# A spectral mixer gated by a token MLP: a buffer for PSUM copies, the order of ScalarE and VectorE before the last stage, and the place of one transform

## The chip, the cores and the metric

The kernel runs on one core of a Trainium2 chip. A core has a matrix engine (TensorE, "PE" in the profile), whose weight loads run beside its matmuls ("PEld"), a vector engine (VectorE, "DVE"), a scalar engine (ScalarE, "ACT"), a general engine (GpSimd, "POOL") and a queue engine (SyncE, "SP"). Each engine works through its own instructions in order; between engines there are only semaphores. SP and POOL also issue the DMA transfers. The metric is the device time of one execution in microseconds; the median over runs is compared.

## The reference

The input is x, 2048 tokens by 512 channels, fp32. It is normalized over the channels once. Two branches start from there: a filter in the Fourier domain over tokens and channels, and an MLP over the tokens (with a second normalization ahead of it). The second branch gates the first.

```python
xn = _layernorm(x, axis=-1)
# filter
X = jnp.fft.rfft2(xn, axes=(-2, -1)) * (w_r + 1j * w_i)
s = jnp.fft.irfft2(X, s=(S, D), axes=(-2, -1))
# token MLP: S = 2048 -> F = 1792 -> S
h = _layernorm(xn, axis=-1)
u = _gelu(jnp.einsum("bsd,sf->bdf", h, w1) + b1)
g = _silu((jnp.einsum("bdf,fs->bds", u, w2) + b2).transpose(0, 2, 1))
return x + s * g
```

## The kernel before

**Tiling.** Token s sits in partition s // 16 and in row j = s % 16, so x is 16 rows of 128 x 512. The Fourier transform over tokens is split into one of length 128 (matmuls against a table) and one of length 16 over the rows. Products of the MLP are made in two parts, high and low, of fp32 values: three matmuls stand for one product (high by high, high by low, low by high). The high part is a rounding copy on ScalarE, the low part a subtraction on VectorE.

**First stage (lines 456 to 520).** The loop over 16 rows makes, in row j, the products of seven of the fourteen 128-wide groups of hidden features with the row's h (line 395; `hidden_early`, lines 392 to 400, four groups to PSUM banks 0 to 3, then three to banks 4 to 6). Between the second and third pass of the first four groups stands `between()`: the row's transform of length 128, four matmuls into bank 7 (`first_transform`, lines 223 to 227). ScalarE copies bank 7 out (`first_copy`, line 231), and `fold` (lines 234 to 250) adds and subtracts pieces of the copy zt into the columns of ey: o, e and two halves of t on VectorE, two groups of ey on GpSimd, one copy of o to the other half of the partitions on ScalarE (line 244), the other two groups of ey on VectorE (line 247). `fold` is a generator: `first_copy` of row j is issued at the end of row j, its folds a row later. For the last row they are issued behind the loop, at line 520, behind the gelus of groups 2 and 1 and behind the first high and low parts of the next weights.

**Middle stage (lines 525 to 751).** The other seven groups and the filter are interleaved by a string of steps, `STEPS`; each letter advances one stream. The first step of the filter is `along_channels`, four matmuls per unit (line 586) that read ey and write bank 4 + q; the units run in the order q = 3, 2, 1, 0. Banks 4, 5 and 6 hold products of the first stage until their gelus have read them.

**Take-over to the last stage (lines 754 to 849).** The last four groups' products still run on TensorE, four parts at a time: `rest(units, gelu)` issues units of products and then the gelu of the group that they complete. Meanwhile the weights w2 of the last stage are loaded and split into high and low parts. The last product is a Strassen-like scheme of seven products for each of eight pairs of output rows (j, j + 8), in the order 1, 2, 5, 6, 3, 7, 4. For each product there is a weight form (`w2_forms`, lines 783 to 812; `w2_form` is one ScalarE copy and one VectorE subtraction, 128 x 896 each): form 1 from the tile a12, 2 from a11, 5 from s1, 6 from s1 + a12, 3 from that + a11, 7 from s4, 4 from a21. On the other side the hidden values u of group pair i, four quarters, are split and summed by `forms(i)` (lines 302 to 327) in five steps: fd (form 1), fa (forms 2 and 3), four sums on VectorE, fc (forms 6 and 5), fb (forms 4 and 7). The last two pairs, 5 and 6 (`last` and `last6`), are made at the take-over. There `strict` is set, and `ordered` keeps an instruction behind the one that was written before it for the same engine. An instruction that is not kept can be put by the scheduler wherever its engine would otherwise stand idle.

**Last stage (lines 854 to 978).** Product n of pair p adds up 21 matmuls (line 941) in one of the banks `bx`, `by`, `bz`. `copied` (line 894) copies a bank's partial sum out on ScalarE, because the next product goes on adding into the same bank: products 1, 6, 7 and 4 share `bx`, and p1 is what stood there after product 1. `sequence` (line 866) and `channels` (line 875) are the last transforms of the filter, `gate` the silu, `finish` the last multiplication and the write.

**Buffers.** Tiles come from pools, which lie on a left and a right side of the memory; a pool that is opened where another was closed lies over its tiles, and each tile then waits for the last readers of the tiles that it overlaps. The pool "us" holds the three tiles u of the hidden values, "w1" the weights of the first two stages; "fin", of the last stage, lies over both. Its first tile is p1. The pool "w2" lies over the middle stage's "mid".

**Loads.** `s1`, `a12`, `a11`, `s4`, `a21` are 448 KB pieces of w2 (line 764); s1 and s4 are sums of two pieces, the second added by a DMA that accumulates (line 766, issued by POOL). The pieces of the next pair are loaded into the same tiles as soon as those are read.

Of the kernel before, what the change touches and what calls it, by code (L numbers as in the profile page):

```python
# [8 lines left out]
F32 = mybir.dt.float32  # L9
# [109 lines left out]
def spectral_mixer_kernel(tc, x, w1, b1, w2, b2, wk, we, wx, c_f, c_ft, c_d, c_i, c_g, c_h, c_s, out):  # L119
# [22 lines left out]
    with tc.tile_pool(name="ps", bufs=1, space=PSUM) as psp, ExitStack() as left, ExitStack() as right:  # L142
# [80 lines left out]
        def first_transform(h, c):  # L223
            z = ps[:, 7].rearrange("p (b c) -> p b c", c=P)
            for b in range(4):
                T.matmul(z[:, b], h[:, b * P:(b + 1) * P], c, start=True, stop=True)  # L226
            return z
# [58 lines left out]
        def gelu(ft, bank):  # L286
            i, half = ft % NH, ft // NH
            if i not in raw:
                raw[i] = usp.tile([P, 2, D], F32, name=f"u{i}", tag="u")
            ordered(A.activation(raw[i][:, half], ps[:, bank], AF.Gelu_apprx_tanh, bias=b1t[:, ft:ft + 1]))  # L290
# [101 lines left out]
        def hidden_early(j, nf, bank, w, between):  # L392
            def products(wi, hj, first, last):
                for i in range(nf):
                    T.matmul(ps[:, bank + i], w[wi][:, i * P:(i + 1) * P], hj, start=first and j == 0, stop=last and j == NJ - 1)  # L395
            products(0, hh[j], True, False)
            products(1, hh[j], False, False)
            r = between()
            products(0, hl[j], False, True)
            return r  # L400
# [56 lines left out]
        for j in range(NJ):  # L457
            more = j + 1 < NJ
            if more:
                raws[j + 1, 0], raws[j + 1, 1] = w1_load(j + 1, *WA), w1_load(j + 1, *WB)  # L460
            if j == 0:
                load_x(3)
                load_x(4)
                SY.dma_start(b1t, b1)
                SY.dma_start(b2t, b2)
            if j == 4:
                SY.dma_start(cd, c_d)
                G.dma_start(cft, c_ft)
            if j in (6, 8, 10, 12):
                q = slice(16 * (j - 6), 16 * (j - 4))  # L470
                SY.dma_start(out[q, :NJ - 1], x[q, :NJ - 1])
            z = hidden_early(j, 4, 0, w[0], lambda: first_transform(h, c))
            hidden_early(j, 3, 4, w[1], lambda: None)

            early = j > 0
            if more:
                w = w1_tiles(j + 1, *WA), w1_tiles(j + 1, *WB)
                h = new_h(j + 1)
                normed(h, xs[j + 1], *of[j + 1])
                high(hh[j + 1], h)  # L480
                if early and j + 3 < NJ:
                    stats(of[j + 3][0], of[j + 3][1], xs[j + 3])
                    if j % 2 == 0:
                        spreads(of[j + 2][0], 2)
            for _ in range(3):
                next(folds, None)
            if more:
                high(w[0][0], raws[j + 1, 0])
            next(folds, None)
            if more:  # L490
                if early and j % 2 == 0 and j + 2 < NJ:
                    scales(of[j + 2][0])
                low(w[0][1], raws[j + 1, 0], w[0][0])
                if not early:
                    stats(m, 0, xs[2])
                high(w[1][0], raws[j + 1, 1])
                low(hl[j + 1], h, hh[j + 1])
                c = turned(j + 1, *of[j + 1])
                if not early:
                    stats(m, 1, xs[3])  # L500
                    spreads(m, 2)
            run(folds)
            if more:
                low(w[1][1], raws[j + 1, 1], w[1][0])
                if not early:
                    scales(m)
                if j % 2 == 0 and j + 4 < NJ:
                    m = moments(f"m{j + 4}", 2)
                    of.update({j + 4: (m, 0), j + 5: (m, 1)})
            if j + 5 < NJ:  # L510
                load_x(j + 5)
            folds = fold(j, first_copy(j, z))
            if j == NJ - 2:
                for i in range(3):
                    w1_raw(i)
        gelu(2, 2)
        w1_high(0)
        w1_low(0)
        gelu(1, 1)
        run(folds)  # L520
        w1_high(1)
        rstage.close()

# [229 lines left out]

        V, A, G, SY = free
        w2p = pool(right, "right", "w2", 3)
        NP, HD = NJ // 2, D // 2
        ORDER = (1, 2, 5, 6, 3, 7, 4)

# [24 lines left out]
        def w2_forms():  # L783

            for p in range(NP):
                yield w2_form(f"1_{p}", cur["a12"])
                yield w2_form(f"2_{p}", cur["a11"])
                w = w2_form(f"5_{p}", cur["s1"])
                ordered(V.tensor_add(cur["s1"], cur["s1"], cur["a12"]))
                yield w  # L790
                w = w2_form(f"6_{p}", cur["s1"])
                if p == 0:
                    yield w
                if p + 1 < NP:
                    nxt["s1"] = s1_load(p + 1, (w2p, fp)[(p + 1) % 2])
                    nxt["a12"] = w2_load("a12", w2p, p + 1, 1)
                if p:
                    yield w
                V.tensor_add(cur["s1"], cur["s1"], cur["a11"])  # L799
                w = w2_form(f"3_{p}", cur["s1"])  # L800
                if p + 1 < NP:
                    nxt["a11"] = w2_load("a11", w2p, p + 1, 0)
                yield w
                w = w2_form(f"7_{p}", cur["s4"])
                if p + 1 < NP:
                    nxt["s4"] = w2_load("s4", w2p, p + 1, 1, (p + 1 + NP, 1))
                yield w
                w = w2_form(f"4_{p}", cur["a21"])
                if p + 1 < NP:
                    nxt["a21"] = w2_load("a21", fp, p + 1 + NP, 0)  # L810
                    cur.update(nxt)
                yield w
# [2 lines left out]

        wforms = w2_forms()
        strict.append(True)
        ready = [next(wforms) for _ in range(3)]

        def rest(units, *gelus):  # L820
            for _ in range(units):
                next(streams["h"])
            for _ in gelus:
                next(streams["g"])
        rest(SPLIT, 5)
        rest(4, 12)
        last, last6 = forms(5), forms(6)
        next(last)
        next(last)
        rest(4, 13)  # L830
        rest(4, 6)
        next(last6)
        next(last)
        next(last6)
        next(last6)
        next(last)
        next(last6)
        ready.append(next(wforms))
        run(last)
        run(last6)  # L840
        strict.clear()
        lstage.close()
        fp = pool(left, "left", "fin", 1)
        HW = [P, HD]
        made = {"p1_0": fp.tile(HW, F32, name="p1_0", tag="p1")}
        gs = [fp.tile([P, D], F32, name=f"g{j}", tag="g", bufs=3) for j in (0, NP)]
        made["c11_0"] = fp.tile(HW, F32, name="c11_0", tag="c", bufs=2)
        made["od0"] = fp.tile([P, 2, P], F32, name="od0", tag="od")
# [43 lines left out]
            return y  # L892

        def copied(name, src):
            t = made.pop(name, None) or fp.tile([P, HD], F32, name=name, tag=name.split("_")[0])
            A.activation(t, src, AF.Copy)  # L896
            return t

# [117 lines left out]
```

## Time and profile before

| | us |
|---|---|
| median of 3 runs | 381.93 |
| lowest, highest | 381.85, 384.48 |
| the profiled execution | 382.29 |
| its span, from the first to the last instruction | 380.5 |
| TensorE busy in it | 369.8 |
| VectorE busy | 309.0 |
| ScalarE busy | 213.3 |
| GpSimd busy | 102.3 |

The profile is one execution, and all its times count from the start of its span. Several views of it are used below: the page with sums by engine; the waits, where a line names the waiting engine and line of code, the engine and line that released it, the total, the number of times and the longest; stretches of time with the busy time of each engine; and the timeline, one line for one or more like instructions in a row, with start, length, engine, line, operation, the tiles written and read, and in brackets the idle time before it and what ended it. "SPq" and "POOLq" are the queues of the two engines that issue DMAs. Lines in a helper that records every operation of an engine are shown as L128. The matmuls overlap, so the end of a row of them is modelled.

The three stages by these times: the first stage to about 98 us, the middle stage to 204.5, the last to the end.

### The profile page before, as it was taken

How to read it: one execution, taken by the hardware profiler on the slowest of the kernel's cores; microseconds unless marked ns; L12 is line 12 of the kernel's file. 1: busy time of each engine (PE TensorE's matmuls, PEld its weight loads, DVE VectorE, ACT ScalarE, POOL GpSimd, SP SyncE). 2: the span in 40 equal slices, each digit the busy share in tenths (PEclk: the TensorE clock that was granted, in tenths of full speed). 3: DMA queues.
4: the chain of work that ended last, by engine and by line, in shares of the span. 5: the costliest groups of instructions: out<-in, count | busy, mean ns of one | idle time of the engine just before them, and what ended most of it. 6: DMA issues, size and time to landing. Idle time of an engine off the chain costs nothing.

```text
span 380.5 us, 7482 instructions
## 1 busy us (share of the span) xinstructions
PE 369.8 (97%) x2760; PEld 327.8 (86%) x2760; DVE 309.0 (81%) x660; ACT 213.3 (56%) x384; POOL 102.3 (27%) x133
## 2 busy tenths in 40 slices
PE   8999999999999999999999799999999999999994
PEld 4888888888877676777779799999999999999994
DVE  5899999865799999999967798776767768777763
ACT  4677755754972365865456765545555555545541
POOL 2133233243511735765400011020303020200100
PEclk9999999999999999999999999999999999999999
DMA  7956467214455767999866599898888888895602
GB/s 249 323 190 231 133 222 239 91 42 128 120 196 179 253 213 258 283 280 307 194 181 155 149 267 188 265 164 263 168 246 184 223 204 193 194 217 158 100 0 56
DMA packets 41945, 73.32 MB, mean 193 GB/s; under 512 B 4180, under 2 KB 25172, under 8 KB 41780
## 3 DMA queue, kind: packets, MB, share of 16 engines
q1 hardware_dynamic: 35460, 58.88, 48.6%
q0 software_dynamic: 6448, 13.96, 21.4%
q8 instruction: 21, 0.34, 0.4%
q14 instruction: 16, 0.13, 0.1%
HBM read 60.24 MB, written 8.13 MB: 180 GB/s over the span
## 4 chain that ended last, share of the span: by engine, by line
PE 86%; DVE 8%; issue 2%; ACT 2%; DMA 1%; SPq 0%; DVEq 0%; ACTq 0%
PE ps L941 34%; PE ps L395 19%; PE ps L678 6%; PE ps L679 5%; PE ps L226 4%; PE ps L687 4%; PE ps L866 4%; PE ps L586 4%; PE ps L875 4%; DVE pq L128 2%; DVE e L128 2%; PE ps L665 1%; PE ps L681 1%; PE ps L600 1%; DMA x<-in_x_dram 1%
## 5 line engine op out<-in xcount | busy, mean ns | idle before, releaser
L395 PE MATMUL ps<-h,w1h 128*128 128x512 f32 x224 | 58.5, 398 | 0.0
L395 PEld LDWEIGHTS ps<-h,w1h 128*128 128x128 f32 x224 | 40.8, 188 | 8.1 <-ACT w1h L387 0.2
L776 DVE TENSOR_TENSOR w2f<-s,w2f 128x896 fp32r<-128x896 f32 x32 | 35.0, 1092 | 14.8 <-ACT w2f L775 13.7
L766 POOL DMA_DIRECT2D s<-in_w_dram x16 | 13.8, 865 | 122.7 <-DMA s<-in_w_dram 35.0
L678 PE MATMUL ps<-h,w1h 128*128 128x512 f32 x112 | 44.9, 401 | 0.0
L679 PE MATMUL ps<-h,w1h 128*128 128x512 f32 x112 | 43.7, 390 | 0.0
L941 PE MATMUL ps<-fb,w2f 128*128 128x256 f32 x336 | 42.9, 282 | 0.6 <-DVE c L904 0.6
L941 PE MATMUL ps<-fa,w2f 128*128 128x256 f32 x336 | 43.4, 283 | 0.0
L941 PE MATMUL ps<-fc,w2f 128*128 128x256 f32 x336 | 41.1, 279 | 2.1 <-ACT p L896 2.1
L941 PEld LDWEIGHTS ps<-fc,w2f 128*128 128x128 f32 x336 | 40.1, 188 | 2.3 <-ACT p L896 2.3
L941 PEld LDWEIGHTS ps<-fb,w2f 128*128 128x128 f32 x336 | 40.6, 188 | 1.4 <-issue 0.8
L941 PEld LDWEIGHTS ps<-fa,w2f 128*128 128x128 f32 x336 | 40.6, 188 | 0.0
L775 ACT ACTIVATE w2f<-s 128x896 fp32r<-128x896 f32 x32 | 30.3, 948 | 16.5 <-DVE s L799 13.5
L776 DVE TENSOR_TENSOR w2f<-a,w2f 128x896 fp32r<-128x896 f32 x24 | 26.1, 1089 | 15.8 <-ACT w2f L775 15.7
L128 POOL TENSOR_TENSOR s<-z,e 128x4 f32<-128x4 f32 x8 | 25.3, 3163 | 37.4 <-DMA z<-e 16.6
L775 ACT ACTIVATE w2f<-a 128x896 fp32r<-128x896 f32 x24 | 22.8, 950 | 21.7 <-PE ps L941 18.2
L395 PE MATMUL ps<-h,w1l 128*128 128x512 f32 x112 | 30.7, 390 | 0.1
L128 ACT ACTIVATE w1h<-w1s 128x512 fp32r<-128x512 f32 (+1 forms) x30 | 17.4, 581 | 22.2 <-PE ps L679 12.9
L678 PEld LDWEIGHTS ps<-h,w1h 128*128 128x128 f32 x112 | 21.0, 188 | 9.0 <-issue 5.0
L687 PE MATMUL ps<-h,w1l 128*128 128x512 f32 x93 | 25.6, 391 | 0.1
L395 PEld LDWEIGHTS ps<-h,w1l 128*128 128x128 f32 x112 | 20.9, 188 | 5.0 <-DVE w1l L390 0.5
L679 PEld LDWEIGHTS ps<-h,w1h 128*128 128x128 f32 x112 | 21.1, 188 | 4.0
(132 smaller groups left out, 730.8 us busy)
## 6 DMA issues: line engine op xcount, KB each, us to landing
a<-in_w_dram SPq DMA_DIRECT2D x24, 448.0 KB
s<-in_w_dram POOLq DMA_DIRECT2D x17, 448.0 KB, 7.0
s<-in_w_dram SPq DMA_DIRECT2D x15, 448.0 KB
w1r<-in_w_dram SPq DMA_DIRECT2D x16, 256.0 KB
z<-e SPq DMA_DIRECT2D x16, 256.0 KB
w1s<-in_w_dram SPq DMA_DIRECT2D x16, 256.0 KB
yj<-ey SPq DMA_DIRECT2D x16, 256.0 KB
x<-in_x_dram SPq DMA_DIRECT2D x15, 256.0 KB
```

Source lines behind the costliest of these rows:

```text
L128: return lambda *a, **k: keep(getattr(engine, name)(*a, **k))
L226: T.matmul(z[:, b], h[:, b * P:(b + 1) * P], c, start=True, stop=True)
L395: T.matmul(ps[:, bank + i], w[wi][:, i * P:(i + 1) * P], hj, start=first and j == 0, stop=last and j == NJ - 1)
L586: keep(T.matmul(pd[:, b * P:(b + 1) * P], ey[:, lo, b].rearrange("p h j -> p (h j)"), cd[:, b], start=True, stop=True))
L678: keep(T.matmul(o, wh[:, sl], hh[j], start=first, stop=False))
L679: keep(T.matmul(o, wh[:, sl], hl[j], start=False, stop=False))
L687: keep(T.matmul(ps[:, bank], wl[:, k * P:k * P + P], hh[j], start=False, stop=final))
L775: ordered(A.activation(wf[:, 0], v, AF.Copy))
L776: ordered(V.tensor_sub(wf[:, 1], v, wf[:, 0].bitcast(F32)))
L866: in_turn(j, T.matmul(pf[:, b], yj[:, b * P:(b + 1) * P], cft, start=True, stop=True))
L875: in_turn(j, T.matmul(pe[:, b % 2, b // 2], yt[:, b], ci[:, b], start=True, stop=True))
L941: in_turn(j0, T.matmul(o, wf[:, wi, i], ui, start=m + a == 0 and n in (1, 2, 5), stop=m == NH - 1 and a == 2, skip_group_check=n in (6, 3, ...
```

## The change

Three edits are in the diff.

1. In the last row of the first stage the transform is issued before the row's products instead of between them, and its folds are issued before the gelus of groups 2 and 1 instead of behind them.
2. p1, the copy of product 1's partial sum, gets a tile of its own in the pool "w2" (a 1 KB buffer per partition, the pool's first tile), for all eight pairs, and leaves "fin".
3. The order in which ScalarE's and VectorE's work is written at the take-over is another. Form 5 of w2 stands behind the gelu of group 5; the sums of u5 stand before the gelus of groups 13 and 6; the order behind the last gelu is fd6, fc5, fa6, then s1 + a12, the sums of u6, form 6 of w2, fc6, fb5, fb6. Before it was fd6, the sums of u5, fa6, the sums of u6, fc5, fc6, form 6, fb5, fb6, with s1 + a12 ahead of all of it. In `w2_forms` the sum s1 + a12 becomes part of the step of form 6, in every pair.

```diff
-            z = hidden_early(j, 4, 0, w[0], lambda: first_transform(h, c))
+            if more:
+                z = hidden_early(j, 4, 0, w[0], lambda: first_transform(h, c))
+            else:
+                z = first_transform(h, c)
+                hidden_early(j, 4, 0, w[0], lambda: None)
             hidden_early(j, 3, 4, w[1], lambda: None)
...
+        run(folds)
         gelu(2, 2)
         w1_high(0)
         w1_low(0)
         gelu(1, 1)
-        run(folds)
         w1_high(1)
...
         w2p = pool(right, "right", "w2", 3)
+        p1_0 = w2p.tile([P, D // 2], F32, name="p1_0", tag="p1", bufs=1)
...
-                w = w2_form(f"5_{p}", cur["s1"])
+                yield w2_form(f"5_{p}", cur["s1"])
                 ordered(V.tensor_add(cur["s1"], cur["s1"], cur["a12"]))
-                yield w
+                if p == 0:
+                    yield
                 w = w2_form(f"6_{p}", cur["s1"])
                 if p == 0:
                     yield w
...
-        ready = [next(wforms) for _ in range(3)]
+        ready = [next(wforms) for _ in range(2)]
...
         rest(SPLIT, 5)
+        ready.append(next(wforms))
         rest(4, 12)
         last, last6 = forms(5), forms(6)
-        next(last)
-        next(last)
+        for _ in range(3):
+            next(last)
         rest(4, 13)
         rest(4, 6)
         next(last6)
         next(last)
         next(last6)
-        next(last6)
-        next(last)
+        next(wforms)
         next(last6)
         ready.append(next(wforms))
+        next(last6)
         run(last)
         run(last6)
...
-        made = {"p1_0": fp.tile(HW, F32, name="p1_0", tag="p1")}
+        made = {"p1_0": p1_0}
...
-            t = made.pop(name, None) or fp.tile([P, HD], F32, name=name, tag=name.split("_")[0])
+            tag = name.split("_")[0]
+            t = made.pop(name, None) or (fp, w2p)[tag == "p1"].tile([P, HD], F32, name=name, tag=tag, bufs=1)
             A.activation(t, src, AF.Copy)
```

## The prediction

> **What bounds the kernel now.** The first view is the page: busy time of each engine in one profiled execution.
>
> ```profile
> span 380.5 us, 7482 instructions
> PE 369.8 (97%) x2760; PEld 327.8 (86%) x2760; DVE 309.0 (81%) x660; ACT 213.3 (56%) x384; POOL 102.3 (27%) x133
> ```
>
> TensorE is busy for 369.8 of 380.5 us, and the change removes no matmul. All that can be won is idle time of TensorE, 10.7 us in all, so the next view is its waits, and after it the busy time in stretches (columns: stretch, length, then PE, PEld, DVE, ACT and POOL busy, clock, DMA share, GB/s).
>
> ```profile
> PE ps L941 <- ACT p L896: 2.1, 1, 2.1
> PE ps L665 <- DVE pq L128: 1.2, 2, 0.7
> PE ps L586 <- DVE ey L247: 0.4, 1, 0.4
> ```
>
> ```profile
> 100.00:130.00 30.00, 29.87 (x227) 23.15 (x226) 29.36 (x52) 17.30 (x32) 8.92 (x11) 1.00 0.60 190
> 204.50:217.00 12.50, 10.39 (x88) 10.15 (x87) 10.15 (x18) 7.36 (x12) 0.86 (x1) 1.00 0.63 173
> 251.00:367.00 116.00, 116.00 (x989) 115.48 (x988) 86.40 (x166) 59.01 (x99) 17.43 (x20) 1.00 0.79 186
> ```
>
> Two of these waits lie where the diff works. The take-over to the last stage holds the largest, 2.1 us, for p1's copy; the start of the filter holds 0.4 us for the last columns of ey. Between the two VectorE is as full as TensorE (29.36 of 30), and behind 251 us TensorE never waits. A gain at either place can therefore be carried to the end by TensorE, if no new wait catches it.
>
> **The last row.** In time order, the end of the first stage (start, length, engine, line, tiles, count):
>
> ```profile
> 91.76 1.75 PE L395 MATMUL ps<-h,w1h 128*128 128x512 f32 x7
> 94.25 1.05 PE L226 MATMUL ps<-cf,h 128*128 128x128 f32 x8
> 95.34 0.60 ACT L231 ACTIVATE zt<-ps 128x512 f32<-128x512 f32 x1 [2.61 <-PE ps L226]
> 95.96 1.28 ACT L290 ACT_TABLE_LOAD   x1
> 97.07 0.46 DVE L240 TENSOR_TENSOR t<-o 64x128 f32<-64x128 f32 x1
> 97.25 1.27 ACT L290 ACTIVATE u<-ps,b1t 128x512 f32<-128x512 f32 x2
> 98.55 0.31 ACT L244 ACTIVATE o<-o 64x128 f32<-64x128 f32 x1
> 98.60 0.60 PE L586 MATMUL ps<-cd,ey 128*128 128x128 f32 x4
> 98.89 0.88 DVE L247 SCALAR_TENSOR_TENSOR ey<-t,o 128x128 f32<-128x128 f32 x2 [1.36 <-ACT o L244]
> 99.31 1.83 ACT L128 ACTIVATE u<-ps,b1t 128x512 f32<-128x512 f32 x3
> 99.57 1.63 PE L586 MATMUL ps<-cd,ey 128*128 128x128 f32 x12 [0.37 <-DVE ey L247]
> ```
>
> The seven matmuls at 91.76 are three of row 14 and the first four of row 15, at 0.227 each (1.59 to the next group, by 7), so row 15 begins at 92.44. Its transform now stands behind eight matmuls, at 94.25, and moves to 92.44: 1.81 earlier, its bank having been free since row 14's copy. The products keep their total. The copy zt goes from 95.34 to 93.53, and VectorE's last t ends at 97.53 − 1.81 = 95.72. The copy o, which now queues behind the table load and two gelus, follows at once (the folds stand ahead of the gelus in the new text) and ends near 96.05; L247 ends near 97.0 instead of 99.77. The wait at 99.57 goes. A 128-wide matmul takes 0.111 by this row of the chain that ended last:
>
> ```profile
> 217.04 0.89 PE ps L866 x8
> ```
>
> Four of L586 from 98.60 would reach 99.05, so the stall is worth 0.52.
>
> What is late next? ScalarE. The table load moves behind o, from 95.96 to 96.05; the two gelus end near 98.61 (98.52 before), the copy o (0.31, a step of 0.33 with its gap) no longer follows them, so the next gelus start at 99.07 instead of 99.31, 0.24 earlier. The second unit of L586 overwrites a bank that the first of those gelus reads; at 0.64 each (1.27 by 2) it ends at 99.71, while the matmuls would be ready at 99.49 (eight at 0.111). So 0.22 of the 0.52 turns into a new wait, and **0.3** is left. If the scheduler lets the first gelu pass o instead (its bank is ready near 95.9, o near 95.72), the load hides in the idle time behind zt and all 0.5 is won. I take 0.3, with ends 0 and 0.5, because the order of the text gives it. Nothing below zero: no work is added. Whether 0.3 lasts to 204 us depends on VectorE, which is full; its copies out of L586 and its forms move with TensorE and ScalarE by the same amount.
>
> [...]
>
> **The take-over.** The same view, some 100 us later:
>
> ```profile
> 203.45 0.33 SPq L764 DMA_DIRECT2D a<-in_w_dram  x1
> 203.83 1.38 SPq L853 DMA_DIRECT2D yj<-ey  x2
> 205.79 0.62 ACT L295 ACTIVATE fa<-u 128x512 fp32r<-128x512 f32 x1
> 205.93 0.42 DVE L296 TENSOR_TENSOR fd<-u,fd 128x256 fp32r<-128x256 f32 x1 [1.60 <-ACT fd L295]
> 208.70 0.42 DVE L315 TENSOR_TENSOR u<-u 128x256 f32<-128x256 f32 x1
> 209.65 2.63 PE L941 MATMUL ps<-fc,w2f 128*128 128x256 f32 x21
> 210.42 1.29 DVE L296 TENSOR_TENSOR fc<-u,fc 128x512 fp32r<-128x512 f32 x2
> 211.63 1.08 DVE L776 TENSOR_TENSOR w2f<-s,w2f 128x896 fp32r<-128x896 f32 x1
> 212.63 1.28 DVE L296 TENSOR_TENSOR fb<-u,fb 128x512 fp32r<-128x512 f32 x2
> 213.95 0.66 ACT L896 ACTIVATE p<-ps 128x256 f32<-128x256 f32 x2 [1.36 <-DVE fb L296]
> 214.39 2.65 PE L941 MATMUL ps<-fc,w2f 128*128 128x256 f32 x21 [2.11 <-ACT p L896]
> 214.43 0.86 POOL L766 DMA_DIRECT2D s<-in_w_dram  x1 [12.62 <-DVE fb L296]
> 215.94 1.09 DVE L776 TENSOR_TENSOR w2f<-s,w2f 128x896 fp32r<-128x896 f32 x1 [0.68 <-ACT w2f L775]
> 217.69 2.72 PE L941 MATMUL ps<-fa,w2f 128*128 128x256 f32 x21
> 218.74 0.58 ACT L868 ACTIVATE yt<-ps 128x512 f32<-128x512 f32 x1
> ```
>
> Product 6 of pair 0 (214.39) adds into the bank of product 1, so it waits for p1's copy. That copy waits for the last fb at 213.91: p1_0 lies where u of tile 6 lay. The other inputs of product 6 were there at 212.71 (its weights, L776). With p1_0 in w2's pool the copy needs only product 1, done long before, and its place: its tile comes first in its pool and lies over middle-stage tiles last used before 200 us, and the pool's other tiles keep theirs.
>
> *The buffer alone.* Product 6 starts at 212.75, 1.64 earlier. Product 3 (217.69, which is 3.30 after product 6, a transform between) would be ready at 216.05, but its weights are done at 217.03 and the third matmul needs them, 0.24 in: it starts near 216.8. Gain 0.9.
>
> *The new order.* From 205.93 VectorE's queue was fd6, four sums of u5, fa6, four sums of u6, fc5, fc6, w2f 6, fb5, fb6, L799. Now u5's sums stand before gelu 13 and run while VectorE waited (1.60 us idle before 205.93), and the sum s1 + a12, which ran ahead of this window, takes their room. With steps of 0.60 for a 512-wide form, 1.01 for an 896-wide one and 1.72 for four sums (208.70 to 210.42): fc5 follows ScalarE at 206.43, fa6 207.03, s1 + a12 207.63, u6's sums 208.64, w2f 6 210.36 (done 211.44), fc6 211.37 (done 212.06), fb5 and fb6 to 213.26, L799 213.17, then ScalarE's copy and w2f 3 at about 215.3, 0.65 before the 215.94 of now. Product 5 uses fc6's low part in its twentieth matmul, at 209.65 + 19/21 of 2.63 = 212.03: a new wait of under 0.1. Product 6 starts at 212.35, two us earlier. Product 3 is ready at 215.65 and waits for w2f 3, done 216.39, to near 216.15 in its first matmul: **1.5 gained**. Behind it the next in line is yt at 218.74, whose ScalarE queue moves by the same 0.65 and ends at 218.67; its reader comes behind product 3, some 2.5 on, at 218.65. That just fits. The upper end is the whole wait, 2.1; the lower end is 0.9, the buffer alone.
>
> *Other edits, at nothing.* w2f 5 behind one gelu is needed only at 209.65. In the other seven pairs the sum s1 + a12 is issued one product later, with no VectorE work between in the text; two products (2.63 each) cover it, and without that cover it would cost 1.08 a pair. fin is 1 KB shorter and its tiles slide; the u and w1 tiles below are dead by then in either place. The load of the next a12 must wait for the moved sum: 208.7 instead of 203.45, past yj and s on SP's queue. It is first read by pair 1's forms, behind the yt of 218.74 on ScalarE, some 10 us after.
>
> **The sum.** 0.3 + 1.5 = 1.8 us. The profiled execution took 382.29 us around its span of 380.5, which is 0.36 above the median of the runs, 381.93; it would go to 380.5, the median to **380.1**. A measurement can tell some 1% here, 3.8 us, and this is half of that.
>
> **Rivals.**
> 1. *SP's queue turns it slower.* Now the a12 load stands first on SP's queue, then the two yj, a21, s1. If it keeps that place, all wait for the moved sum, 5.2 us later than 203.45. Then s1's second half, which POOL issues at 214.43, goes out near 219.7 and lands 7.0 us on (the median in the row below), at 226.7, or later, since more loads then leave together. w2f 5 of pair 1 needs it, and yt of ScalarE stands behind that:
>
> ```profile
> s<-in_w_dram POOLq DMA_DIRECT2D x17, 448.0 KB, 7.0
> 224.75 0.95 ACT L775 ACTIVATE w2f<-a 128x896 fp32r<-128x896 f32 x1 [1.93 <-PE ps L941]
> 226.49 0.60 ACT L868 ACTIVATE yt<-ps 128x512 f32<-128x512 f32 x1
> 228.77 1.05 PE L875 MATMUL ps<-cd,yt 128*128 128x128 f32 x8
> ```
>
> With the 1.5 won, the reader L875 would come at 227.3; from the start of w2f 5 to the end of yt it is 2.3 (224.75 to 227.09), so s1 must be there by 225.0. A landing at 226.7 costs 1.7. With 9.0 us instead of 7.0 it costs 3.7, which is 1.9 slower than now: 383.8. The point from which it is slower than before is 226.8. Against it: the loads go in the order in which they can start, and yj can start at once. Chance 0.08.
> 2. *The first part costs.* The load behind o takes longer, or drains: the gelu that L586 awaits ends some 1.3 later (the load's own length once more), at 101.0, against the 100.01 at which that unit starts now (99.57 and four matmuls). 1.0 lost, 1.5 won: 381.4. The 0.01 us between load and gelu speaks against it. Chance 0.08. [...]
> 3. *All waits go.* 0.5 and 2.1 are won in full, and VectorE's earlier start eats part of the 1.2 that L665 waits for pq: 379.3, at most 378.1. The full VectorE speaks against it. Chance 0.10.
> 4. *Nothing happens:* ScalarE still takes p1's copy up behind the last fb and another input is as late: 381.9. The weights at 212.71 against 214.39 speak against it. Chance 0.08.
>
> **How the numbers follow.** My forecast has 0.66, with its own range 379.2 to 381.0 (gains of 0.9 to 2.7). The range 378.8 to 382.2 takes in rivals 2 and 4 and most of 3, and leaves out rival 1 and the far end of 3, under 0.2 with the errors of both. Faster by over 1%, under 378.1: 0.06, from rival 3. Slower by over 1%, over 385.7: 0.04, rival 1 at twice its price. The rest, 0.90, is within 1%.
>
> **What would show it.** The transform of the last row 1.8 us earlier, o ahead of the table load, no wait of L586 for L247, perhaps one for a gelu of some 0.3. At the take-over p1's copy before fb, product 6 two us nearer to product 5 than before, and a short wait of product 3 for L776. A wait of ScalarE for a or s near 218 to 227, or SP standing at L764 with yj behind it, would make me wrong, and so would a wait of L941 for p that remains.

## The result

| | before | after |
|---|---|---|
| median, us (12 runs each, side by side) | 382.23 | 380.89 |
| lowest, highest | 381.85, 384.48 | 380.13, 381.88 |
| the profiled execution | 382.29 | 380.93 |
| its span | 380.5 | 379.1 |

The ratio is 0.9947, with a 95% interval from 0.9928 to 0.9965. The change gains about half a per cent. It is less than the 1% named as what a measurement can tell, but here the interval keeps clear of 1.

The page and the waits of TensorE after the change:

```profile
span 379.1 us, 7480 instructions
PE 370.6 (98%) x2760; PEld 328.3 (87%) x2760; DVE 310.1 (82%) x660; ACT 212.8 (56%) x384; POOL 101.3 (27%) x133
```

```profile
PE ps L384 <- POOL wz L372: 1.3, 1, 1.3
PE ps L669 <- DVE pq L128: 1.2, 2, 0.7
PE ps L949 <- DVE w2f L781: 0.2, 1, 0.2
```

TensorE has 2760 matmuls, as before. The two waits at which the change was aimed, 2.1 us of the last products for p1's copy and 0.4 us for ey, are gone, and a short one for w2f (L781 is L776 of before) is new. The wait for pq has stayed at 1.2. The stretch of the take-over, by the same columns as before:

```profile
204.50:217.00 12.50, 12.22 (x100) 11.74 (x99) 9.57 (x15) 7.99 (x13) 0.00 (x0) 1.00 0.45 125
```

TensorE is now busy for 12.22 of 12.50 us, where it was 10.39.

**The last row**, in time order:

```profile
92.80 1.05 PE L226 MATMUL ps<-cf,h 128*128 128x128 f32 x8
96.17 0.31 ACT L244 ACTIVATE o<-o 64x128 f32<-64x128 f32 x1 [1.68 <-DVE t L240]
96.50 1.28 ACT L290 ACT_TABLE_LOAD   x1
96.51 1.56 DVE L247 SCALAR_TENSOR_TENSOR ey<-t,o 128x128 f32<-128x128 f32 x2 [0.43 <-ACT o L244]
97.79 1.27 ACT L290 ACTIVATE u<-ps,b1t 128x512 f32<-128x512 f32 x2
98.53 0.19 PEld L682 LDWEIGHTS ps<-h,w1h 128*128 128x128 f32 x1 [0.31 <-ACT u L290]
98.53 0.50 PE L682 MATMUL ps<-h,w1h 128*128 128x512 f32 x1
99.11 2.15 PE L590 MATMUL ps<-cd,ey 128*128 128x128 f32 x16
104.59 0.71 PE L604 MATMUL ps<-ey,gf 32*32 32x512 f32 x16
```

The row now begins with its transform, so it begins at 92.80; in the kernel before it began at 92.44 (the prediction's working). Its end is taken to be the first matmul of the filter's next step, at 104.59 here. In the kernel before that matmul stands here:

```profile
104.52 0.71 PE L600 MATMUL ps<-ey,gf 32*32 32x512 f32 x16
```

From start to end it was 12.08 us, and now it is 11.79: 0.29 less.

**The take-over:**

```profile
204.81 2.64 PE L949 MATMUL ps<-fd,w2f 128*128 128x256 f32 x21
207.48 0.38 ACT L904 ACTIVATE p<-ps 128x256 f32<-128x256 f32 x1 [0.44 <-PE ps L949]
207.76 1.08 DVE L794 TENSOR_TENSOR s<-s,a 128x896 f32<-128x896 f32 x1
208.91 0.33 SPq L769 DMA_DIRECT2D a<-in_w_dram  x1
209.29 1.46 SPq L860 DMA_DIRECT2D yj<-ey  x2
209.75 5.45 PE L949 MATMUL ps<-fc,w2f 128*128 128x256 f32 x42
210.48 1.08 DVE L781 TENSOR_TENSOR w2f<-s,w2f 128x896 fp32r<-128x896 f32 x1
212.22 2.78 PEld L949 LDWEIGHTS ps<-fc,w2f 128*128 128x128 f32 x23 [0.28 <-DVE fc L296]
215.04 1.05 PE L873 MATMUL ps<-cft,yj 128*128 128x128 f32 x8
215.39 1.09 DVE L781 TENSOR_TENSOR w2f<-s,w2f 128x896 fp32r<-128x896 f32 x1 [0.69 <-ACT w2f L780]
216.54 2.50 PE L949 MATMUL ps<-fa,w2f 128*128 128x256 f32 x19 [0.21 <-DVE w2f L781]
218.19 0.59 ACT L875 ACTIVATE yt<-ps 128x512 f32<-128x512 f32 x1
218.88 1.11 PE L882 MATMUL ps<-cd,yt 128*128 128x128 f32 x8
219.53 0.85 POOL L771 DMA_DIRECT2D s<-in_w_dram  x1 [19.29 <-DVE w2f L781]
228.60 0.95 ACT L780 ACTIVATE w2f<-s 128x896 fp32r<-128x896 f32 x1 [0.47 <-DMA s<-in_w_dram]
```

p1 is copied (207.48) as soon as product 1 is through; products 5 and 6 follow each other from 209.75 in a row of 42 matmuls; product 3 stops for 0.21 us after two matmuls. From the start of product 1 to the first transform over the channels (L882, L875 of before) it is 14.07 us here. Product 1 of the kernel before:

```profile
204.70 2.63 PE L941 MATMUL ps<-fd,w2f 128*128 128x256 f32 x21
```

That transform came 2.56 behind the start of product 3 (217.69), at 220.25, which makes 15.55 us. The take-over gained 1.48.

What is left of idle time there shows in the starts, since the end of a row is modelled. Products 1 and 2 take 2.47 us each to the start of the next, products 5 and 6 together 5.29 (209.75 to 215.04): 0.35 more than twice 2.47. It lies at the weight load at 212.22, which waits for fc. Product 3 takes 3.03 (215.85 to 218.88) against 2.56 in the kernel before, so its stop costs 0.47.

**The account.** 0.29 and 1.48 are 1.77 us. The span is only 1.4 shorter, since the first matmul of the hidden products (row 0's) stands at 7.30 after the change and at 6.33 before it: over the eleven other profiles of this case it lies anywhere from 6.16 to 6.92. From there to the end it is 371.80 against 374.17, 2.37 less. The 0.6 beyond the two places lies in the rows of the first stage, which the change does not touch: from that first matmul to the filter's next step it took 97.60 in one and 98.19 in another profile with the same code there. In all, the last row begins 0.36 us later than before (92.80 against 92.44), which turns 1.77 into 1.4.

Nor does the change reach the start: TensorE begins with 16 matmuls of L384, and their steps halve from 0.43 to 0.22 us where the trace's record of full clock begins, at 4.79 us before the change and at 6.81 after it. The first hidden matmul comes at 6.33 and at 7.30. In the six profiles where it comes at 6.58 or later (e10_fill's aside, where it first waits 0.50 for h) it is 85.50 to 85.52 us from there to the last row, in the five where it comes at 6.42 or earlier 85.78 to 86.13: the rows take back part of an early start.

### The profile page after: what moved, and what is told of

Read it like the earlier page. It is cut to its first block, busy times and chain, and to the rows that moved or that the text cites. A ratio compares the mean times of both kernels' runs of the same rounds, so it can differ in the third digit from the quotient of the medians.

```text
span 379.1 us, 7480 instructions
## 1 busy us (share of the span) xinstructions
PE 370.6 (98%) x2760; PEld 328.3 (87%) x2760; DVE 310.1 (82%) x660; ACT 212.8 (56%) x384; POOL 101.3 (27%) x133
## 4 chain that ended last, share of the span: by engine, by line
PE 83%; DVE 11%; issue 3%; ACT 1%; POOL 1%; DVEq 0%; POOLq 0%
PE ps L949 33%; PE ps L395 20%; PE ps L682 4%; PE ps L683 4%; PE ps L226 4%; PE ps L882 4%; PE ps L873 4%; DVE pq L128 3%; PE ps L590 3%; DVE e L128 3%; PE ps L691 3%; PE ps L384 2%; PE ps L669 1%; PE ps L685 1%; DVE w2f L781 1%
## 5 line engine op out<-in xcount | busy, mean ns | idle before, releaser
L781 DVE TENSOR_TENSOR w2f<-s,w2f 128x896 fp32r<-128x896 f32 x32 | 34.9, 1092 | 15.2 <-ACT w2f L780 14.3
L682 PE MATMUL ps<-h,w1h 128*128 128x512 f32 x112 | 45.0, 402 | 0.0
L781 DVE TENSOR_TENSOR w2f<-a,w2f 128x896 fp32r<-128x896 f32 x24 | 26.0, 1089 | 13.7 <-ACT w2f L780 13.7
L682 PEld LDWEIGHTS ps<-h,w1h 128*128 128x128 f32 x112 | 21.0, 188 | 9.2 <-issue 5.0
```

What stands on the lines that cost most here:

```text
L682: keep(T.matmul(o, wh[:, sl], hh[j], start=first, stop=False))
L781: ordered(V.tensor_sub(wf[:, 1], v, wf[:, 0].bitcast(F32)))
```

## The experiments

The table holds what the profiles of all kernels show at the two places, and their times. "Row" is the way from the first matmul of the last row to the filter's next step, "take-over" the way from product 1 to the first transform over the channels, "rest" from there to the end of the span.

| kernel | row | take-over | rest | span | median (runs) | ratio to before, 95% |
|---|---|---|---|---|---|---|
| before | 12.08 | 15.55 | 160.25 | 380.5 | | |
| after | 11.79 | 14.07 | 160.22 | 379.1 | 380.89 (12) | 0.9928 to 0.9965 |
| e1_row | 11.78 | 17.16 | 160.18 | 381.6 | 383.5 (12) | 0.9978 to 1.0023 |
| e2_buffer | 12.08 | 14.72 | 160.28 | 379.5 | 381.4 (12) | 0.9936 to 0.9975 |
| e3_order | 12.08 | 14.97 | 160.10 | 379.5 | 382.02 (12) | 0.9958 to 0.9998 |
| e4_both | 12.06 | 14.08 | 160.24 | 378.8 | 381.1 (12) | 0.9924 to 0.9969 |
| e10_fill | 12.08 | 15.64 | 161.56 | 382.2 | 382.41 (12) | 0.9959 to 1.0 |
| e5_forms | 11.78 | 13.60 | 160.67 | 378.7 | 381.25 (12) | 0.9924 to 0.9965 |
| e7_folds | 11.40 | 14.03 | 160.38 | 378.4 | 380.63 (12) | 0.9919 to 0.9977 |
| e8_all | 11.40 | 13.61 | 160.53 | 378.0 | 380.37 (8) | 0.9903 to 0.9955 |
| e6_sp | 11.80 | 14.08 | 160.33 | 378.5 | 380.31 (5) | 0.9883 to 0.9939 |
| e9_held | 11.77 | 19.74 | 160.14 | 383.9 | 386.04 (10) | 1.0045 to 1.0107 |

Where kernels have the same code in the last row, their ways through it agree within 0.03 us, and those through the take-over within 0.05 (14.03 to 14.08, and 13.60 with 13.61), but for one exception that the first experiment shows; their spans and medians differ by several tenths. So the terms of the sum are read from the ways, and the medians only bound the whole, the more so as the experiments were run in three groups on three chips, each beside the kernel before and not beside the change.

**e1_row: the first edit alone, on the kernel before.**

```diff
+            if more:
+                z = hidden_early(j, 4, 0, w[0], lambda: first_transform(h, c))
+            else:
+                z = first_transform(h, c)
+                hidden_early(j, 4, 0, w[0], lambda: None)
...
+        run(folds)
         gelu(2, 2)
...
-        run(folds)
```

> The kernel before with edit 1 alone (the last row's transform and folds first). My theory: the stall of the first unit of the filter (0.52 us) goes, and about half of it comes back as waits for the gelus, which start later behind the table load. From the first matmul of the last row to the first matmul of the forward transform (12.08 us before, 92.44 to 104.52) it should take 11.8, the rest of the kernel the same, so the time is 0.3 us shorter. Rival, the gelus lose as much as the folds win: 12.1 and no change. Rival, the start of the filter moves VectorE's full middle stage by more: over 0.6 us shorter, with the stretch from the forward transform to product 1 (100.2 us before) shorter too.

The row is 11.78, so the first edit is worth 0.30 by itself. The median shows no gain, and the way through the take-over, where no code differs from before, is 1.61 longer than before. The timeline and the stretches of TensorE (columns: stretch, length, PE busy, clock, DMA share, GB/s) tell why:

```profile
209.21 2.63 PE L945 MATMUL ps<-fc,w2f 128*128 128x256 f32 x21
213.94 4.27 PE L945 MATMUL ps<-fc,w2f 128*128 128x256 f32 x21 [2.10 <-ACT p L900]
```

```profile
209.25:213.75 4.50, 2.59 (x22) 1.00 0.59 187
213.95:214.20 0.25, 0.25 (x1) 0.67 0.00 0
214.45:217.20 2.75, 2.75 (x15) 0.50 0.58 55
217.20:217.70 0.50, 0.50 (x6) 0.75 0.94 229
```

The wait for p1's copy is the same 2.10 us as before. But behind it the granted clock is 0.50, and product 6 takes 4.27 us instead of 2.65. These 1.62 are the whole difference of 1.61. The clock in the second and fourth of the stretches shown places the change: at full clock for a third of 213.95 to 214.20, and again for half of 217.20 to 217.70. So it fell near 214.03 and rose near 217.45, 3.4 us in all. In the profiled execution of before the same wait was followed by full clock.

**e2_buffer: the second edit alone.**

```diff
+        p1_0 = w2p.tile([P, D // 2], F32, name="p1_0", tag="p1", bufs=1)
...
-        made = {"p1_0": fp.tile(HW, F32, name="p1_0", tag="p1")}
+        made = {"p1_0": p1_0}
...
```

> The kernel before with p1's buffer in w2's pool alone, the old order of ScalarE and VectorE. My theory: product 6 waits for its own weights (VectorE done at 212.7) instead of p1's copy, and product 3 then waits for its weights at 217.0. From the start of product 1 to the first matmul of the first channel transform (15.55 us before, 204.70 to 220.25) it should take about 14.7, so 0.9 us shorter. Rival, the buffer is all of the gain and the order nothing: 14.1, 1.5 us shorter. Rival, the copy stays behind fb and nothing changes: 15.5.

The take-over is 14.72: the buffer alone is worth 0.83. The timeline shows the two stops that are left, both for weight forms:

```profile
212.57 2.43 PE L943 MATMUL ps<-fc,w2f 128*128 128x256 f32 x19 [0.25 <-DVE w2f L777]
216.88 1.33 PE L943 MATMUL ps<-fa,w2f 128*128 128x256 f32 x9 [0.63 <-DVE w2f L777]
```

**e3_order: the third edit alone.** p1 stays in "fin", over the tile u of group 6. The beginning of the diff at the take-over is shown; the rest is the third edit as above.

```diff
-        ready = [next(wforms) for _ in range(3)]
+        ready = [next(wforms) for _ in range(2)]
...
+        ready.append(next(wforms))
         rest(4, 12)
         last, last6 = forms(5), forms(6)
-        next(last)
-        next(last)
+        for _ in range(3):
+            next(last)
...
```

> The kernel before with the new order of ScalarE and VectorE alone, p1 still over tile u of the last group. My theory: fb ends about 0.6 us earlier and p1's copy with it, so product 6 starts 0.6 earlier; product 3's weights are then no limit. From product 1 to the first channel transform 14.9 to 15.0 instead of 15.55, 0.6 us shorter. Rival, the order is most of the gain: 14.1 to 14.4. Rival, the order alone does nothing: 15.5.

The take-over is 14.97: the order alone is worth 0.58. p1's copy still stands behind the last fb, but fb comes earlier, and the wait shrinks from 2.1 to 1.1:

```profile
213.46 2.74 PE L943 MATMUL ps<-fc,w2f 128*128 128x256 f32 x21 [1.12 <-ACT p L898]
```

**e4_both: the second and third edit, without the first.** Its diff is that of the change without the hunks of e1_row.

> The kernel before with buffer and order, without edit 1. My theory: from product 1 to the first channel transform 14.1, as in the changed kernel, and 1.5 us shorter than before; the stretch from the last row to the forward transform stays at 12.1. The two parts add up almost: 0.9 and 0.6. Rival, one of them makes the other useless: the same as the better one alone.

The take-over is 14.08 and the row 12.06. So the two edits make 1.47 together, close to the sum of 0.83 and 0.58, and the places are independent: the first edit changes nothing at the take-over, and these two nothing in the row.

**e10_fill: the kernel before, with 17 matmuls in the wait.** They write an unused part of bank 7 and are read by nothing. They stand behind product 5 of the first pair.

```diff
+                if p == 0 and n == 5:
+                    for i in range(17):
+                        in_turn(j0, T.matmul(ps[:, 7, :HD], wf[:, 0, i % NH], uh, start=True, stop=True))
```

> The kernel before with 17 more matmuls (2.0 us) between products 5 and 6 of pair 0, which write a bank that nobody reads: TensorE works through most of the 2.1 us in which it waited for p1's copy. In the row experiment's profile the granted clock fell to half for 3.4 us behind that wait, and in some half of the executions of the kernel before the time is near 384.2 instead of 382.0. Theory, the clock falls because of the idle time: with it filled no execution shows a mean clock under 0.997 or a time over 383.3, and the median is near 382.1, some 1.5 to 2 us below that of the kernel before over all its executions, though work was added. Rival, the wait has nothing to do with the slower executions: half of them stay near 384.

The take-over is 15.64, 0.09 longer than before. What was idle is filled, and product 6 starts no earlier, 4.74 behind product 5 (209.95 to 214.69), as in the kernel before (209.65 to 214.39). The median is nevertheless 1.45 below that of the kernel before on the same chip (382.41 against 383.86). The reason stands in the mean granted clock that is recorded for each execution. The kernel before is counted over 79 of its 80 executions beside the experiments (one of 2081.53 us is left out):

| kernel | TensorE's waits at the take-over | executions | with a mean clock below 0.997 | their median | median of the others |
|---|---|---|---|---|---|
| before | 2.1 | 79 | 45 | 384.27 | 382.03 |
| e1_row | 2.1 | 12 | 9 | 383.63 | 381.83 |
| e10_fill | the 2.1 filled | 12 | 0 | | 382.41 |
| e3_order | 1.1 | 12 | 0 | | 382.02 |
| e2_buffer | 0.25 and 0.63 | 12 | 0 | | 381.4 |
| e4_both | 0.2 | 12 | 0 | | 381.1 |
| after | 0.2 | 12 | 0 | | 380.89 |
| e9_held (below) | 3.4 | 10 | 6 | 386.49 | 385.22 |

Of the kernels with the same matmuls at this place, those that leave TensorE idle for 2 us or more lose the clock in over half of their executions; those with 1.1 or less, and the one whose wait is filled with matmuls that compute nothing, do so in none of the 60 executions of the table. Of the 37 executions of the four kernels not listed (e5_forms, e6_sp, e7_folds, e8_all), one of e7_folds has a clock of 0.996. The expectation that no execution of e10_fill would take over 383.3 was missed by one, the profiled one, with 383.97 at full clock. In this profile another 1.3 us lie behind the take-over ("rest" 161.56), where TensorE's longest wait for L904 is 1.3; why that wait grew was not tried.

**e5_forms: form 3 moved up as well.** After the change product 3 waits 0.2 for its weights. Here the sum with a11 and form 3 of the first pair stand ahead of the last fb. Because a12 and a11 of the next pair then wait later for those sums, their loads are kept in the place where they are written, behind yj, a21 and s1. Of the diff the new form and the kept loads are shown.

```diff
                 w = w2_form(f"6_{p}", cur["s1"])
                 if p == 0:
                     yield w
+                    ordered(V.tensor_add(cur["s1"], cur["s1"], cur["a11"]))
+                    yield
+                    yield w2_form(f"3_{p}", cur["s1"])
...
-            queue.dma_start(t, w2_half(j, h))
+            load = queue.dma_start(t, w2_half(j, h))
+            if name in ("a12", "a11") and j == 1:
+                keep(load)
...
```

> The changed kernel with the sum s1 + a11 and form 3 of w2 made before the last fb instead of behind the take-over, and the next pair's a12 and a11 loads pinned behind the two yj, a21 and s1 on SP's queue. My theory: product 3 no longer waits for its weights; from product 1 to the first channel transform 13.6 instead of 14.07, 0.45 us shorter. Rival, product 3's weights were not the limit: 14.0 to 14.1. Rival, the copies behind (yt of the first transform) are late next: 13.8 to 14.0 with a wait of L875's line for ScalarE.

The take-over falls to 13.60, 0.47 below the change, which is all that product 3's stop cost; the 0.35 in products 5 and 6 are still there. The rest is 160.67, against 160.10 to 160.38 in the kernels with form 3 in its old place (e10_fill's 161.56 aside), so part of the gain may be given back; but it is 160.53 in e8_all and 160.14 in e9_held, which have form 3 early as well, so that this is not shown. The time is that of the change.

**e7_folds: the change, with the last row's folds behind the gelus again.** Only the transform is early.

```diff
-        run(folds)
         gelu(2, 2)
...
         gelu(1, 1)
+        run(folds)
         w1_high(1)
```

> The changed kernel with the last row's transform first, but its folds issued behind the gelus as before the change. My theory: the table load then runs behind zt in time that is idle anyway, the gelus start at once when their banks are ready, the copy o still comes in time for the first unit of the filter, and the whole 0.5 us is won: from the last row's first matmul to the forward transform 11.6 instead of 11.79 (12.08 before). Rival, the copy o is late again behind the two gelus and holds L247: 11.9 to 12.1.

The row is 11.40, 0.68 below the kernel before and 0.39 below the change:

```profile
92.44 1.05 PE L226 MATMUL ps<-cf,h 128*128 128x128 f32 x8
94.14 1.28 ACT L290 ACT_TABLE_LOAD   x1
96.06 1.27 ACT L290 ACTIVATE u<-ps,b1t 128x512 f32<-128x512 f32 x2 [0.63 <-PE ps L395]
97.35 0.31 ACT L244 ACTIVATE o<-o 64x128 f32<-64x128 f32 x1
98.58 3.73 PE L590 MATMUL ps<-cd,ey 128*128 128x128 f32 x32
```

The table load runs directly behind zt, in time in which ScalarE had nothing else to do, 1.70 us behind the row's start instead of 3.70; the gelus start as soon as their products are there; the copy o behind them is still early enough, with the transform early. So the half of the first edit that moves the folds costs more than it brings. One of the 12 executions took 385.45 at a clock of 0.996; its cause is not known.

**e8_all: e5_forms and e7_folds together.**

> The two last edits together on the changed kernel. My theory: 0.45 + 0.2 = 0.65 us shorter than the changed kernel, some 380.2 in the median. Rival, VectorE's full middle stage takes the 0.2 back: 0.45. Rival, both fail: no difference.

Both ways hold (11.40 and 13.61). The median of 380.37 is 0.5 below that of the change, and the lowest time, 379.78, 0.35 below its lowest. The intervals of the two ratios overlap.

**e6_sp: the change, with the load of a12 kept behind yj, a21 and s1.** This undoes what the moved sum did to SP's queue.

```diff
-            queue.dma_start(t, w2_half(j, h))
+            load = queue.dma_start(t, w2_half(j, h))
+            if name == "a12" and j == 1:
+                keep(load)
```

> The changed kernel with one thing undone: on SP's queue the load of a12 for pair 1 is issued behind the two yj, a21 and s1 again, so these go out near 203.8 as in the kernel before, instead of behind the sum s1 + a12 at 208.9. Theory (SP's queue order cost 0.47 us of ScalarE's time and nothing on TensorE): ScalarE no longer waits 0.47 us for s at 228.6, the way from product 1 to the first channel transform stays 14.0 to 14.1 us, and the time is that of the changed kernel, 380.9 within 0.5. Rival (the late loads of yj and s1 are on the path, as the prediction's first rival had it): that way gets shorter by 0.5 us or more and the time falls to 380.4 or below.

The take-over stays at 14.08. Form 5 of the second pair no longer waits for s, and starts 1.29 earlier than in the change, but 0.72 of that is the earlier start of the whole (product 1 at 204.09 instead of 204.81):

```profile
227.31 0.94 ACT L782 ACTIVATE w2f<-s 128x896 fp32r<-128x896 f32 x1
```

Its profile and the change's agree from the first hidden matmul to the end (371.9 and 371.8 us). The median of five runs, 380.31, lies 0.6 below the change's, which is a little more than the theory's bound and within the rival's; since neither way got shorter, it is not put down to the queue. Order on SP's queue cost ScalarE 0.47 us and TensorE nothing.

**e9_held: e5_forms with the two loads free to go first.**

```diff
-            load = queue.dma_start(t, w2_half(j, h))
-            if name in ("a12", "a11") and j == 1:
-                keep(load)
+            queue.dma_start(t, w2_half(j, h))
```

> The kernel e5_forms (form 3 of pair 0 made as s1 + a12 + a11 at the take-over, ahead of the last fb) without the one thing that kept a12 and a11 of pair 1 behind yj, a21 and s1 on SP's queue: now they stand ahead, and a11 waits for the sum with a11 near 213, about 4 us later than a12's wait in the changed kernel. Theory (a load held up on SP's queue costs only what reaches a reader, and yj has its reader on VectorE and TensorE behind product 3, near 216 to 219): yj now lands at 215.5 or later, the way from product 1 to the first channel transform grows from the 13.6 us of e5_forms by 0.5 to 3 us, and s1's second half lands 4 us later, which ScalarE and then product 5 of pair 1 wait for. The time is 381.5 to 384. Rival (the queue's order does not reach TensorE at all, for all transfers have room): 13.6 us and 381.2 as in e5_forms.

The take-over grows to 19.74, by 6.14 us where the theory allowed 3, and the time to 386.04. SP's queue and TensorE in the timeline, and TensorE's stretches (columns as above):

```profile
208.12 4.65 SPq L769 DMA_DIRECT2D a<-in_w_dram  x2
212.83 1.38 SPq L866 DMA_DIRECT2D yj<-ey  x2
217.84 2.08 PE L879 MATMUL ps<-cft,yj 128*128 128x128 f32 x8 [3.44 <-DMA yj<-ey]
219.57 4.35 PE L955 MATMUL ps<-fa,w2f 128*128 128x256 f32 x21
```

```profile
217.80:219.90 2.10, 2.06 (x9) 0.50 0.93 228
222.50:224.00 1.50, 1.50 (x12) 0.76 0.50 181
```

SP stands for 4.65 us at the loads of a, whose tile the second sum has yet to read. yj goes out at 212.83 and its reader waits 3.44 us, until 217.84, 5.0 us behind the issue. Then the clock is at 0.50, and the transform and product 3 take 2.08 and 4.35 instead of 1.05 and 2.72. 3.44 + 1.03 + 1.63 = 6.10, against the 6.14 by which the way grew. Four of the ten executions kept a mean clock of 0.997 or more and still took 385.22 in the median, 1.27 less than the others; only one of the others is profiled, so how long TensorE waited in the four is not known. A load that waits at the head of a queue does cost what the prediction's first rival was about, as soon as a reader on TensorE is behind it: 3.44 us of waiting here, and 2.66 more at the lower clock. In the change yj goes out at 209.29 and is read at 215.04. With the 5.0 us from here it would land near 214.3, by this estimate with 0.7 us to spare.

## Why the prediction was right

380.1 was predicted, with 378.8 to 382.2 around it; 380.89 was measured. It was right in its mechanism and in the size of the two terms, with luck in the first, and it had one step wrong that cost nothing.

- *The last row, 0.3.* It measured 0.29 here and 0.30 in e1_row. The copy o, L247 and the table load came in the order of the text, as taken: o ends 3.68 behind the row's start (96.48 less 92.80; worked out were 3.61), and the load follows at once. L247 ends at 98.07, 0.7 later from the row's start than worked out, because its two operations take 1.56 where they took 0.88 (below), and yet long before L590 at 99.11; the wait for ey is gone. The gelu that is late took back a part, as foreseen, but at another instruction: L682, a product ahead of L590, whose weight load waits 0.31 for u. L590 comes 0.15 later from the row's start than before (6.31 against 6.16) and the step behind it is 0.44 shorter. The upper end, where the load hides behind zt, was said to need the scheduler; e7_folds shows that it needs only that `run(folds)` stays where it was. It also shows that the agreement to 0.01 us is luck: without the late load the early transform gains 0.68, where the stall was put at 0.52, and the late load takes back 0.39, where 0.22 was worked out. Both sizes were too small by nearly the same.
- *The table load (second rival).* Load and gelu stand at 96.50 + 1.28 and 97.79, and at 95.96 + 1.28 and 97.25 before, so in either order the load took 1.28 and the gelu followed 0.01 behind it. Neither a longer load nor a drain shows.
- *The take-over, 1.5.* 1.48 was measured, with w2f 6 done at 211.56 (211.44 had been worked out), w2f 3 at 216.48 (216.39) and yt at 218.78 (218.67), each 0.09 to 0.12 later, as product 1 itself is (204.81 against 204.70). The buffer alone was put at 0.9 and measured 0.83. So each edit was sized from the right limit: p1's place, then VectorE's queue ahead of w2f 3. One small term was put too low: the "new wait of under 0.1" in product 5 is the 0.35 at the weight load for fc.
- *Not all waits go (third rival).* Product 3 stops for 0.21 us, and the wait for pq is 1.2 as before. e5_forms removes the former, without a gain in the time.
- *SP's queue (first rival, and "other edits").* The loads were said to change places, with a12 "past yj and s on SP's queue". They did not. a12 kept the head of the queue at 208.91, 5.46 later than in the kernel before; yj followed at 209.29, and s1's second half was issued at 219.53 (the rival had 219.7) and held ScalarE until 228.60. So the rival's event came true, and its price of 3.7 us did not. With it came the sign that was to make the prediction wrong, SP at the load with yj behind it, and TensorE lost nothing by it. The step that failed is its reader: the row at 224.75 was read as form 5 of the second pair, although the row itself says `w2f<-a`; form 5 is the copy from s, and in the kernel before it stands later:

```profile
229.34 0.94 ACT L775 ACTIVATE w2f<-s 128x896 fp32r<-128x896 f32 x1
```

  A landing near 228.6 is thus hardly late, and e6_sp shows that it is worth nothing on TensorE. The rival's mechanism is real, as e9_held shows: it decides at yj, not at s, and by the estimate above the change passes it by 0.7 us.
- *The other edits, at nothing.* The moved sum in the other seven pairs cost nothing that the profiles show: from the take-over to the end it is 160.22 against 160.25.
- *The size of the whole.* The sum was 1.8 and the two places give 1.77. The medians differ by 1.34 in the side-by-side runs, where 4 of the 12 executions of the kernel before took 383.89 or more, and by more beside the experiments, where the medians of the kernel before were 383.83, 383.86 and 383.96. What no step of the prediction had is the clock: the profiled execution of before ran at full clock, and 45 of the 79 executions counted above had a mean clock below 0.997. Against before's median at full clock, 382.03, the change's median is 1.14 lower; against the others', 384.27, 3.38. Of the 0.6 between 1.77 and 1.14 nothing is settled; the start alone varies by as much between executions: the last row begins at 92.07 to 92.80 in the twelve profiles, and latest in that of the change.

## What to carry to other kernels

A wait of the bounding engine is worth what stands behind it: follow each input of the waiting instruction to its own end, then the next instruction's, and a change like this can be sized closely; the take-over came out within a tenth of a microsecond, the last row by errors that cancelled. Read the tile names in the row before you say which reader a late load has, and look for the nearest reader on the whole queue behind it, not only for the one of the tile that moved. Measure edits by the way between two fixed instructions of the trace, since the start of the kernel alone moved the last row by up to 0.73 us here (92.07 to 92.80), and look at the granted clock of all executions before you trust the profiled one.

## What the runs showed of the hardware

**The clock.** With an idle time of TensorE of 2.1 us in the midst of full work, over half of the executions had a mean clock below 0.997: 45 of 79 of the kernel before and 9 of 12 of e1_row. In e1_row's profile, which is one of them, 3.4 us at a granted clock of 0.50 followed (214.03 to 217.45), at a price of 1.6 us. In e9_held's, with a wait of 3.44 us, it was about 6.8 us at 0.50, from near 216.4 to near 223.2: the mean clock is 0.92 from 213.00 to 217.00 and 0.76 from 222.50 to 224.00. After an idle time of 1.1 us (e3_order) no execution of 12 had a mean clock below 0.997.

Why the clock falls in some executions and not in others of the same kernel is not shown. In the profile of the kernel before TensorE waited 2.1 us as in e1_row's, and the clock stayed at 1.00; four of the ten executions of e9_held had a mean clock of 0.997 or more.

**VectorE beside GpSimd.** L247's two operations took 1.56 us in the change (96.51 above), 0.88 in the kernel before and 0.62 in e7_folds, on tiles of the same shape. In the change L247 ran from 96.51 to 98.07 and GpSimd was at work until 97.83:

```profile
96.37 0.72 POOL L128 TENSOR_TENSOR wa<-wa 2x256 f32<-2x256 f32 x1
97.06 0.77 POOL L128 TENSOR_TENSOR wb<-wb 2x256 f32<-2x256 f32 x1
```

In e7_folds GpSimd's two were through at 97.43, before L247 began at 97.69. In the kernel before GpSimd's wb ran until 99.23, 0.34 us into L247. The first of L247's operations there, beside wb, took 0.63 us, and the second, beside other operations of GpSimd (e from wet, from 99.19), 0.40; in the change the two took 0.82 and 0.89. So in these three profiles the longer times came with wa and wb and not with GpSimd's work as such. Why is not shown, and it cost nothing at this place: in the change L247 ended at 98.07 and L590 began at 99.11.
